# A two-stage attention and channel mixer: half of one weight matrix converted during the first batch's products, and one maximum on GpSimd

## The chip, the cores and the metric

The kernel runs on one core of a Trainium2 chip. A core has a matrix engine (PE, with its own weight loader), a vector engine (DVE), a scalar engine (ACT), a general engine (POOL, called GpSimd in the code), and SyncE (SP), whose queue issues the transfers here. The metric is device time in microseconds, the median of three timed runs. One more execution is recorded by the hardware profiler; all rows in this document are from such executions.

## What is computed

For each of 8 batches and 8 heads, 32 packed queries `p` attend over 576 keys and values of width 64; the packed result then serves as keys and values for 576 queries `q`. The eight heads side by side give x of 576 tokens by 512 channels. A low-rank mixer adds a term over the tokens, and a two-layer network over the channels follows:

```python
p_packed = sm_attn(p, k, v)
out = sm_attn(q, p_packed, p_packed)
xt = x.transpose(0, 2, 1)
h = xt @ U @ V
u = x + h.transpose(0, 2, 1)
ch = np.maximum(u @ w_ch1, 0.0) @ w_ch2
return u + ch
```

`w_ch1` (w1, 512 by 2048) and `w_ch2` (w2, 2048 by 512), U and V come as float64; the others are float32.

## The kernel before, in words

**Two parts.** The front part (up to line 541) runs the first attention for all batches in 16 units, one for each batch and half of the heads, the second attention of batch 0, and the conversion of all of w1. Its instructions are put in order by a planner that simulates the program and takes, for each engine, what is ready by its costs; instructions traced earlier have precedence. From line 544 on, `tc.manual_schedule()` keeps the order in which the code is written, engine by engine. There, a loop over batches `b` and 16 row blocks `kt` of the hidden layer runs `gemm1(kt)` and then `gemm2(kt - 1)`, and hangs the other work between them. Each engine takes its instructions strictly in the order given.

**Products.** Every float32 factor is split into two parts, and a product is three matmuls (`mm3`, lines 84 to 88). `gemm1` does not multiply by w1 itself: `fold(b, c)` (line 355) first multiplies a quarter of w1's columns by the packed attention of batch b, into tiles `wth`, `wtl`. That takes 16 matmuls into two banks of the two-bank pool `psT`, four ACT copies (L367) and four DVE subtractions (L368). Quarter c = 0 of batch 0 is folded at unit 13, and quarters 1, 2, 3 in the loop at the end of kt = 2, 6, 10; quarter c needs the four converted chunks 4c to 4c + 3 of w1. The two banks are also used by the attention steps and by the leftover steps `rest` of the front part, so a PE step that needs a bank waits until L368 has read the fold's. `gemm1` evicts with ACT (`hh`, L596, and `hj`, L598) and DVE (`hl`, L599); its two banks are single, so `gemm1(kt + 1)` waits for the `hl` of kt.

**Conversion of float64.** `float32_of` (line 71) makes float32 from the two 32-bit words: an absolute value on ACT (L77, or L143 in `test_w1`), a maximum against a constant on DVE (L78), and three DVE instructions on bits: a shift and mask (L79), and two that combine it with the words (L80, L81). w1 comes in 16 chunks of 128 by 512 (512 KB each), loaded by `load_w1`, tested by `test_w1` and converted by `convert_w1`; in the front part one chunk goes with each unit, and two with units 1, 5 and 9. w2 comes in 16 blocks of the same size: blocks 0 to 2 are loaded in the front part, one more is loaded, converted and split (L158 on ACT, L159 on POOL) with each kt of batch 0 up to kt = 13. The tiles of a conversion, `os`, are four in all, shared by w1 and w2.

**Second attention.** `attention(b, res)` is a list of 24 steps: a load of q (two transfers of 576 KB into the two `x` tiles), turns (PE transposes, copies from PSUM half by ACT and half by DVE), scores, softmax (DVE maximum L267, POOL subtraction L268, ACT exponential L271, DVE sum L276, POOL product L279, DVE transpose L283), tokens, and the mixer (`mix1`, `mix2`). In the loop of batch b the steps of batch b + 1 are popped, one after `gemm1` and one at the end of a kt; at kt % 4 == 2 the fold takes the second place. Batch 1's load is issued in the front part, at unit 13; `rest` has the first place in kt = 0 to 3.

Of the kernel before, what the change touches and what calls it, by code (L numbers as in the profile page):

```python
# [19 lines left out]
def packed_attention_mixer_kernel(  # L20
# [27 lines left out]
    nc = tc.nc  # L48
# [22 lines left out]
    def float32_of(x, t, raw, out=None, tested=False):  # L71


        low, high = raw[:, :, 0], raw[:, :, 1]
        out = x if out is None else out.bitcast(I32)
        if not tested:
            nc.scalar.activation(t, high.bitcast(F32), AF.Abs)  # L77
        nc.vector.tensor_single_scalar(t, t, LEAST, op=ALU.max)  # L78
        nc.vector.tensor_scalar(x, t.bitcast(I32), 3, 0x3FFFFFF8, op0=ALU.logical_shift_left, op1=ALU.bitwise_and)  # L79
        nc.vector.scalar_tensor_tensor(x, high, -0x40000000, x, op0=ALU.bitwise_and, op1=ALU.bitwise_or)  # L80
        nc.vector.scalar_tensor_tensor(out, low, 29, x, op0=ALU.logical_shift_right, op1=ALU.bitwise_or)  # L81
        return out.bitcast(F32)
# [47 lines left out]

    chunks = [(x, c) for c in range(NPC) for x in range(4)]
# [9 lines left out]
    def test_w1(n):  # L141
        tests[n] = conv_tile(F32)
        nc.scalar.activation(tests[n], bits["w1", n][:, :, 1].bitcast(F32), AF.Abs)  # L143

# [20 lines left out]

    def x_tile():
        return pipe.tile([P, 5 * 2 * P], F32, name="x", tag="x", bufs=2)
# [32 lines left out]

    def turn(t, x, h, bank):
# [3 lines left out]
        if h < 2:  # L205
# [4 lines left out]
            for a in range(2):  # L210
                dst = t[:, 2 * h:2 * h + 2, :4 * I].rearrange("p z (k i a) -> p a z k i", k=2, a=2)[:, a]
                if a:
                    nc.vector.tensor_copy(dst, src[:, a])
                else:
                    nc.scalar.copy(dst, src[:, a])
# [25 lines left out]
    def attention(b, res):  # L241
# [11 lines left out]
        def turn_q(g, h):  # L253
            if h == 0:
                st["t", g] = pipe.tile([P, 4, 5 * I], F32, name="xT", bufs=1)
            turn(st["t", g], st["x", g], h, bank)
# [240 lines left out]
    n_w1 = 0  # L497
    for i in range(NU):
# [42 lines left out]
    actx.close()  # L541

# [19 lines left out]
    class Batch:  # L562
# [39 lines left out]
        def gemm2(self, kt):  # L602
# [3 lines left out]
            for t in range(4):  # L606
                ts_ = slice(t * P, t * P + P)
# [54 lines left out]

    w2x = convert_w2(1)
    last, parts = None, []
    for b in range(B):
# [3 lines left out]
        for kt in range(NK):  # L669
            cur.gemm1(kt)  # L670
            if oj and kt == 1:
                store_joint(b - 1, oj)
            if rest:
                rest.pop(0)()
            elif steps and (b == 0 or kt % 4 != 2):
                steps.pop(0)()
            if (b, kt) == (0, 5):
                w2_tiles(ctx.enter_context(tc.tile_pool(name="sC", bufs=1, side="right", reuse_waits="tile")), 2)
            if kt > 0:
                cur.gemm2(kt - 1)  # L680
# [5 lines left out]
            if w2x:  # L686
# [57 lines left out]
```

## Time and profile before

| | |
|---|---|
| median of 3 runs | 881.36 us (880.0 to 882.8) |
| the profiled execution's own time | 877.17 us |
| its span, first to last instruction | 875.2 us |
| mean granted clock of PE | 0.973 |
| PE busy | 836.0 us, 96% |
| DVE busy | 402.6 us, 46% |
| ACT busy | 322.8 us, 37% |
| POOL busy | 95.0 us, 11% |
| read from memory, written | 47.79 MB, 10.35 MB |

In a row of a timeline stand the start in us, the duration in us, the engine, the line, the operation and the tiles, and in brackets how long the engine was idle before and what ended that. A row of a table by stage gives the busy time of each engine within the stage with the count of its instructions, then PE's granted clock, the busy share of the transfer engines, and what these moved. A row of groups gives the total and the mean ns of one instruction. PE shows busy when its pipeline is filled, so a PE near 100% is not PE at its peak.

### The profile page before, as it was taken

The page shows a single profiled execution, that of the slowest core. Times are in us where ns is not written, and L with a number is a line of the kernel's source. Part 1 is how long each engine was busy: PE and PEld are TensorE (multiplying, and loading weights), DVE is VectorE, ACT ScalarE, POOL GpSimd, SP SyncE. Part 2 cuts the span into 40 slices and gives each one's busy share as a digit, 9 for nine tenths or more (in the row PEclk, how much of TensorE's full clock was granted, in tenths as well). Part 3 has the DMA queues.
Part 4 walks back from the last instruction along what each step waited for, and adds up shares of the span by engine and source line. Part 5 has one row for each costly group of instructions (what it writes and reads, how often), then busy time and mean ns, then how long its engine had stood idle before and what let it go on. Part 6 is the DMA issues. An engine that isn't in the chain of part 4 may idle for free.

```text
span 875.2 us, 14665 instructions
## 1 busy us (share of the span) xinstructions
PE 836.0 (96%) x5808; PEld 665.1 (76%) x5808; DVE 402.6 (46%) x988; ACT 322.8 (37%) x1000; POOL 95.0 (11%) x111
## 2 busy tenths in 40 slices
PE   5878899979999999999999999999999999999997
PEld 2554557858888888788878878888888887888886
DVE  4699757876433323433443433434343334332221
ACT  3666564534322333234223332233223332332221
POOL 0002222323001100100010000110011001010000
PEclk8799799989999999999999999999999999999999
DMA  8999833322100110011001100011001100010001
GB/s 273 290 337 292 278 115 102 95 75 85 49 1 1 61 53 10 1 61 49 1 1 61 49 13 1 1 61 49 1 1 61 48 13 1 1 49 1 1 1 60
DMA packets 38979, 59.08 MB, mean 68 GB/s; under 512 B 11776, under 2 KB 21888, under 8 KB 38912
## 3 DMA queue, kind: packets, MB, share of 16 engines
q1 hardware_dynamic: 38912, 58.16, 20.4%
q8 instruction: 45, 0.74, 0.4%
q14 instruction: 22, 0.18, 0.1%
HBM read 47.79 MB, written 10.35 MB: 66 GB/s over the span
## 4 chain that ended last, share of the span: by engine, by line
PE 85%; DVE 7%; DMA 4%; issue 1%; ACT 1%; POOL 0%; SPq 0%; ACTq 0%; DVEq 0%; POOLq 0%
PE o L86 16%; PE o L88 16%; PE o L87 16%; PE h_ps L86 8%; PE h_ps L88 7%; PE h_ps L87 7%; PE t_ps L361 4%; DMA bits<-in_moe_w_ch_dram 2%; PE t_ps L208 1%; DVE os L80 1%; PE t_ps L229 1%; PE s_ps L229 1%; PE t_ps L304 1%; PE t_ps L236 1%; DMA x<-in_moe_U_dram 1%
## 5 line engine op out<-in xcount | busy, mean ns | idle before, releaser
L86 PE MATMUL o<-w2h,hh 128*128 128x512 f32 x512 | 208.7, 408 | 0.0
L88 PE MATMUL o<-w2h,hl 128*128 128x512 f32 x512 | 203.5, 397 | 0.0
L87 PE MATMUL o<-w2l,hh 128*128 128x512 f32 x512 | 203.0, 397 | 0.0
L599 DVE SCALAR_TENSOR_TENSOR hl<-h_ps,hh 128x256 fp32r<-128x256 f32 x256 | 104.4, 422 | 167.2 <-ACT hj L598 154.4
L596 ACT ACTIVATE hh<-h_ps 128x256 fp32r<-128x256 f32 x256 | 98.9, 388 | 188.9 <-PE h_ps L88 188.1
L86 PE MATMUL h_ps<-ah,wth 128*128 128x320 f32 (+1 forms) x512 | 158.2, 309 | 1.2 <-DVE hl L599 1.2
L87 PE MATMUL h_ps<-al,wth 128*128 128x320 f32 (+1 forms) x512 | 151.6, 296 | 0.0
L88 PE MATMUL h_ps<-ah,wtl 128*128 128x320 f32 (+1 forms) x512 | 151.4, 296 | 0.0
L86 PEld LDWEIGHTS h_ps<-ah,wth 128*128 128x128 f32 x512 | 96.9, 189 | 32.7 <-issue 25.7
L88 PEld LDWEIGHTS o<-w2h,hl 128*128 128x128 f32 x512 | 97.1, 190 | 23.1
L86 PEld LDWEIGHTS o<-w2h,hh 128*128 128x128 f32 x512 | 97.4, 190 | 22.2 <-issue 4.1
L87 PEld LDWEIGHTS o<-w2l,hh 128*128 128x128 f32 x512 | 97.6, 191 | 17.4
L87 PEld LDWEIGHTS h_ps<-al,wth 128*128 128x128 f32 x512 | 97.0, 189 | 1.9
L88 PEld LDWEIGHTS h_ps<-ah,wtl 128*128 128x128 f32 x512 | 97.0, 190 | 0.0
L368 DVE TENSOR_TENSOR wtl<-t_ps,wth 128x256 fp32r<-128x256 f32 x128 | 48.5, 419 | 93.9 <-ACT wth L367 90.5
L367 ACT CAST wth<-t_ps 128x256 fp32r<-128x256 f32 x128 | 43.4, 374 | 109.1 <-PE t_ps L361 97.1
L324 POOL TENSOR_TENSOR al<-aT,ah 128x320 fp32r<-128x320 f32 (+1 forms) x32 | 26.2, 818 | 211.6 <-ACT ah L323 211.6
L268 POOL TENSOR_TENSOR e<-e,m 128x576 f32<-128x576 f32 x16 | 19.6, 1226 | 237.8 <-DVE m L267 232.4
L361 PE MATMUL t_ps<-w1t,ppT 64*32 64x512 f32 x512 | 36.5, 601 | 0.0
L323 ACT CAST ah<-aT 128x320 fp32r<-128x320 f32 (+1 forms) x32 | 13.9, 433 | 52.8 <-DVE aT L322 52.8
L279 POOL TENSOR_TENSOR e<-e,s 128x576 f32<-128x576 f32 x16 | 18.9, 1179 | 110.3 <-DVE s L278 106.4
L296 DVE TENSOR_TENSOR x<-t_ps,x 128x512 fp32r<-128x512 f32 (+1 forms) x24 | 14.3, 599 | 32.6 <-ACT x L295 32.6
(130 smaller groups left out, 1021.9 us busy)
## 6 DMA issues: line engine op xcount, KB each, us to landing
bits<-in_moe_w_ch_dram SPq DMA_DIRECT2D x32, 512.0 KB, 4.9
kx<-in_k_dram SPq DMA_DIRECT2D x16, 576.0 KB, 6.1
x<-in_q_dram SPq DMA_DIRECT2D x16, 576.0 KB, 4.8
vt<-in_v_dram SPq DMA_DIRECT2D x64, 128.0 KB, 4.9
out_dram<-bits SPq DMA_DIRECT2D x32, 256.0 KB, 2.4
pn<-in_p_dram SPq DMA_DIRECT2D x16, 64.0 KB, 5.6
vt<-in_v_dram SPq DMA_DIRECT2D x16, 64.0 KB, 4.2
out_dram<-os SPq DMA_DIRECT2D x8, 128.0 KB, 2.3
```

Of the source, the lines that this page charges most:

```text
L86: nc.tensor.matmul(ps, lhsT=lh, rhs=rh, start=start, stop=False)
L87: nc.tensor.matmul(ps, lhsT=lh, rhs=rl, start=False, stop=False)
L88: nc.tensor.matmul(ps, lhsT=ll, rhs=rh, start=False, stop=stop)
L229: nc.tensor.matmul(ss[r][hs, :n], lhsT=lT[rs, g, hs], rhs=t[rs, h, :n], start=True, stop=True)
L268: nc.gpsimd.tensor_tensor(e, e, m.unsqueeze(2).to_broadcast([P, S // 32, 32]), op=ALU.subtract)
L279: nc.gpsimd.tensor_tensor(e, e, s.unsqueeze(2).to_broadcast([P, S // 32, 32]), op=ALU.mult)
L324: nc.gpsimd.tensor_tensor(al[:, g, ns], aT[:, ns], ah[:, g, ns].bitcast(F32), op=ALU.subtract)
L361: nc.tensor.matmul(f_ps[g][xs], lhsT=ppT[b][zs, g, xs], rhs=w1t[h // 2][zs, QW * c:QW * c + QW], start=True, stop=True)
L367: nc.scalar.copy(hi[:, g], f_ps[g][:, cs])
L368: nc.vector.tensor_tensor(lo[:, g], f_ps[g][:, cs], hi[:, g].bitcast(F32), op=ALU.subtract)
L596: nc.scalar.activation(hh[:, ms], src, AF.Relu)
L599: nc.vector.scalar_tensor_tensor(hl[:, ms], src, 0.0, hh[:, ms].bitcast(F32), op0=ALU.max, op1=ALU.subtract)
```

## The change

Chunks 0 to 7 of w1 (column quarters 0 and 1) stay in the front part, one with every second unit. The loads of chunks 8 to 10 are traced at unit 14; chunks 8 to 15 are converted in the loop of batch 0 by `late_w1`, two each at kt = 0, 2 and 4 and one each at kt = 1 and 3. They are loaded into tiles that the second attention uses, the two `x` tiles and `xT`, so the q load of batch 1 comes after them. Batch 1's attention starts, load and all, when the last chunk is converted, at the end of kt = 4, and has three places in each kt then (after `gemm1`, in the middle of `gemm2`, at the end), two where a fold stands. The maximum of all 16 chunks of w1 goes from DVE to GpSimd, behind the absolute value. In the loop, both PSUM copies of a turn are on ACT.

```diff
         if not tested:
             nc.scalar.activation(t, high.bitcast(F32), AF.Abs)
-        nc.vector.tensor_single_scalar(t, t, LEAST, op=ALU.max)
+            nc.vector.tensor_single_scalar(t, t, LEAST, op=ALU.max)
...
+    EARLY = 8
...
     def load_w1(n):
         x, c = chunks[n]
-        b = bits["w1", n] = bits_tile() if n % 2 else sA.tile([P, 512, 2], I32, name="bits2")
+        if n < EARLY:
+            b = bits_tile() if n % 2 else sA.tile([P, 512, 2], I32, name="bits2")
+        else:
+            b = xT_tile().rearrange("p h x -> p (h x)") if (n - EARLY) % 3 == 2 else x_tile()
+            b = b[:, :2 * QW].bitcast(I32).rearrange("p (x t) -> p x t", t=2)
+        bits["w1", n] = b
...
         nc.scalar.activation(tests[n], bits["w1", n][:, :, 1].bitcast(F32), AF.Abs)
+        nc.gpsimd.tensor_single_scalar(tests[n], tests[n], LEAST, op=ALU.max)
...
-                if a:
+                if a and split_copies:
                     nc.vector.tensor_copy(dst, src[:, a])
                 else:
                     nc.scalar.copy(dst, src[:, a])
...
     def some_w1(n):
         convert_w1(n)
-        if n + 1 < 16:
+        if n + 1 < EARLY:
             test_w1(n + 1)
-        if n + 4 < 16:
+        if n + 4 < EARLY:
             load_w1(n + 4)
...
-        for _ in range(2 if i in (1, 5, 9) else 1):
-            if n_w1 < 16:
-                some_w1(n_w1)
-                n_w1 += 1
+        if i % 2 == 1:
+            some_w1(i // 2)
...
         if i == 13:
             fold(0, 0)
-            steps = attention(1, res)
-            steps.pop(0)()
         if i == 14:
             split_w2(*convert_w2(0))
             load_w2(2)
+            for n in range(EARLY, EARLY + 3):
+                load_w1(n)
...
+    split_copies = False
...
-        def gemm2(self, kt):
+        def gemm2(self, kt, between=None):
...
             for t in range(4):
+                if t == 2 and between:
+                    between()
...
+    def late_w1():
+        nonlocal n_w1
+        n = n_w1
+        convert_w1(n)
+        for m, f in ((n + 1, test_w1), (n + 3, load_w1)):
+            if m < len(chunks):
+                f(m)
+        n_w1 += 1
+
+    n_w1 = EARLY
+    test_w1(n_w1)
     w2x = convert_w2(1)
+    steps = attention(1, res)
...
+            def step():
+                if steps and (b > 0 or n_w1 == len(chunks)):
+                    steps.pop(0)()
+
             cur.gemm1(kt)
...
             if rest:
                 rest.pop(0)()
-            elif steps and (b == 0 or kt % 4 != 2):
-                steps.pop(0)()
+            elif b == 0 or kt % 4 != 2:
+                step()
+            if b == 0 and kt < 5:
+                late_w1()
...
             if kt > 0:
-                cur.gemm2(kt - 1)
+                cur.gemm2(kt - 1, step if b == 0 else None)
...
+            if b == 0 and kt in (0, 2, 4):
+                late_w1()
             if kt % 4 == 2 and (b, kt) != (B - 1, NK - 2):
                 n = b * NPC + kt // 4 + 1
                 fold(n // NPC, n % NPC)
-            elif steps:
-                steps.pop(0)()
+            else:
+                step()
```

More of the change, by code (lines that the diff above doesn't have):

```diff
@@ L129, in bits_tile, with x_tile, xT_tile @@
         return pipe.tile([P, 512, 2], I32, name="bits", bufs=2)
+    def x_tile():
+        return pipe.tile([P, 5 * 2 * P], F32, name="x", tag="x", bufs=2)
+    def xT_tile():
+        return pipe.tile([P, 4, 5 * I], F32, name="xT", bufs=1)
     chunks = [(x, c) for c in range(NPC) for x in range(4)]
+    EARLY = 8
     bits = {}
@@ L164, in packed_attention_mixer_kernel @@
     vs = const.tile([P, S], F32R, name="vs")
-    def x_tile():
-        return pipe.tile([P, 5 * 2 * P], F32, name="x", tag="x", bufs=2)
     def load_uv():
@@ L199, in load_nat @@
             in_=src[b, 4 * g:4 * g + 4].rearrange("(h z) (i c) d -> (z i) h (c d)", z=2, c=NT))
+    split_copies = True
     def turn(t, x, h, bank):
@@ L254, in turn_q @@
             if h == 0:
-                st["t", g] = pipe.tile([P, 4, 5 * I], F32, name="xT", bufs=1)
+                st["t", g] = xT_tile()
             turn(st["t", g], st["x", g], h, bank)
@@ L491, in some_w1 @@
         convert_w1(n)
-        if n + 1 < 16:
+        if n + 1 < EARLY:
             test_w1(n + 1)
-        if n + 4 < 16:
+        if n + 4 < EARLY:
             load_w1(n + 4)
-    n_w1 = 0
     for i in range(NU):
```

## The prediction

> **What bounds the kernel now.** I read the busy time by stage first, and then the chain of waits inside the stage that looked worst.
>
> ```profile
> core 0: us, PE busy (x) PEld busy (x) DVE busy (x) ACT busy (x) POOL busy (x), PEclk, DMA share, GB/s
> 0.00:120.00 120.00, 94.12 (x1121) 56.12 (x1121) 88.03 (x242) 70.42 (x214) 16.86 (x30) 0.84 0.88 277
> 40.00:80.00 40.00, 32.16 (x476) 20.74 (x473) 37.77 (x104) 26.35 (x79) 6.56 (x8) 0.92 0.96 309
> 100.00:110.00 10.00, 6.62 (x57) 4.74 (x55) 8.30 (x16) 5.70 (x19) 4.97 (x5) 0.72 0.91 290
> 122.00:208.00 86.00, 79.07 (x581) 64.76 (x571) 64.15 (x129) 41.13 (x116) 24.51 (x26) 0.96 0.32 104
> 420.00:520.00 100.00, 99.73 (x614) 81.78 (x612) 37.89 (x93) 31.74 (x100) 7.87 (x8) 1.00 0.08 27
> ```
>
> There are three regimes. In the front part (0 to 122) two things are full at once in the middle: DVE with 37.77 of 40 us, and the transfers with a share of 0.96 at 309 GB/s. PE is idle for 26 of the first 120 us and runs at a clock of 0.84. In batch 0 (122 to 208 is its kt = 0 to 14) PE is idle for 7 us and DVE is 75% busy. From batch 1 on PE has 99.73 of 100, and nothing beside PE matters.
>
> So the change takes work from a stage where DVE and the transfers bound, and puts it into one where PE nearly bounds but where DVE's queue already stops it now and then. The first stage's chain, from 60 to 125, with one of its stretches in order of time (start, duration, what):
>
> ```profile
> by line: PE s_ps L229 12.0%; DMA bits<-in_moe_w_ch_dram 11.6%; DVE os L80 7.4%; PE m_ps L236 6.1%; PE k_ps L208 5.6%; DVE w1t L81 5.3%; DVE mx L433 5.1%; PE m_ps L463 5.1%; DVE os L79 4.3%; DVE os L78 4.0%; DVE kT L213 3.3%; DMA ppTd<-ppTa
> 93.86 7.54 DMA bits<-in_moe_w_ch_dram
> 101.42 0.67 ACT os L77
> 105.96 0.73 DVE mx L433 x2
> ```
>
> The conversions (L78 to L81) hold 21.0% of these 65 us, 13.7 us. From 93.86 on the chain is the load of w2's block 1 and its conversion; the maximum of the next unit (105.96) stands behind it on DVE.
>
> **The front part: what goes.** The groups, by shape, from 0 to 260; one row on the turns of k (ns of one at least, in the middle and at most, first and last start); and two transfer rows (size, us to landing):
>
> ```profile
> L80 DVE SCALAR_TENSOR_TENSOR os<-bits,os 128x512 int32<-128x512 int32 x32 | 23.9, 746 | 0.6
> L78 DVE TENSOR_SCALAR os<-os 128x512 f32<-128x512 f32 x32 | 20.9, 653 | 12.5 <-ACT os L77 8.5 <-ACT os L143 3.8
> L79 DVE TENSOR_SCALAR os<-os 128x512 int32<-128x512 int32 x32 | 15.4, 480 | 1.4
> L81 DVE SCALAR_TENSOR_TENSOR w1t<-bits,os 128x512 int32<-128x512 int32 x16 | 11.4, 713 | 0.0
> L143 ACT ACTIVATE os<-bits 128x512 f32<-128x512 f32 x16 | 10.9, 678 | 7.9 <-DMA bits<-in_moe_w_ch_dram 6.1 <-DVE w1t L81 0.9 <-DVE mx L433 0.7
> L159 POOL TENSOR_TENSOR w2l<-os,w2h 128x512 fp32r<-128x512 f32 x16 | 21.0, 1315 | 39.3 <-ACT w2h L158 39.3
> L466 POOL COPY ppall<-two 128x64 f32<-128x64 f32 x16 | 5.9, 368 | 82.7 <-ACT two L465 82.7
> L208 PE MATMUL k_ps<-ident,kx x128: 272/273/475, 5.9 to 109.7; 128*128 128x128 f32 x128
> bits<-in_moe_w_ch_dram SPq DMA_DIRECT2D x32, 512.0 KB, 4.9
> x<-in_q_dram SPq DMA_DIRECT2D x16, 576.0 KB, 4.8
> ```
>
> Eight chunks leave: 8 x 512 KB = 4.19 MB, at the 0.30 MB per us of the stage 14.0 us of transfer time. On DVE they are 8 x (0.653 + 0.480 + 0.746 + 0.713) = 20.7 us, and the maxima of the eight that stay are 8 x 0.653 = 5.2 us more. Both full resources get more than 14 us, so the smaller, the transfers, says 14. To this comes a second part. `test_w1(8)` now stands ahead of `convert_w2(1)` on ACT, and its load comes last in the front part, so w2's block 1 is converted later, where DVE is free: the chain loses the 4.5 us from 101.42 to 105.96. That makes 18.5. Batch 1's q load also leaves (2 x 576 KB), but behind the last k it delayed nothing on the chain, and I give it 0; if it did delay something, it would be 1.18 MB, 3.9 us.
>
> The bounds: at least half of the conversions' 13.7 us in the chain, so 7. At most what PE allows: it is idle for 26 us, some 6 of these before the first turn (5.9), so 20. I take **17**, near what the transfers say. The three late loads at unit 14 come when the share has fallen and cost nothing; in front of the last units they would cost 3 x 0.52 / 0.30 = 5.2 us (the last rival).
>
> The GpSimd maximum is not in the trace. It reads one tensor of 512 columns: more than the copy of 64 columns (0.368), less than the subtraction of two tensors of 512 (1.315). I take the middle, 0.8. In the front part POOL has 103 of 120 us free, which hides 8 x 0.8; what it costs in batch 0 comes below.
>
> **Batch 0, kt = 0 to 3.** Rows of PE (the first `gemm1` and its end, two `gemm2` with their ends, the waits, and the `gemm1` of kt = 6 and 14), then of DVE:
>
> ```profile
> 122.36 0.42 PE L86 MATMUL h_ps<-ah,wth 128*128 128x320 f32 x1
> 124.15 0.90 PE L463 MATMUL t_ps<-vt,eT 128*32 128x64 f32 x40
> 129.34 0.48 PE L86 MATMUL o<-w2h,hh 128*128 128x512 f32 x1
> 132.18 0.60 PE L208 MATMUL t_ps<-ident,x 128*128 128x128 f32 x4
> 141.63 0.30 PE L473 MATMUL t_ps<-ident,two 128*128 128x128 f32 x1 [0.59 <-DVE wtl L368]
> 158.04 0.39 PE L86 MATMUL h_ps<-ah,wth 128*128 128x320 f32 x1
> 184.78 0.41 PE L86 MATMUL h_ps<-ah,wth 128*128 128x320 f32 x1 [1.23 <-DVE hl L599]
> 190.46 1.08 PE L236 MATMUL t_ps<-ident,aT 128*128 128x128 f32 x4 [3.83 <-DVE wtl L368]
> 191.20 0.77 PE L86 MATMUL o<-w2h,hh 128*128 128x512 f32 x1
> 196.47 0.62 PE L236 MATMUL t_ps<-ident,aT 128*128 128x128 f32 x4
> 208.12 0.38 PE L86 MATMUL h_ps<-ah,wth 128*128 128x320 f32 x1
> ```
>
> ```profile
> 125.36 0.75 DVE L599 SCALAR_TENSOR_TENSOR hl<-h_ps,hh 128x256 fp32r<-128x256 f32 x2 [3.35 <-ACT hj L598]
> 127.13 1.06 DVE L78 TENSOR_SCALAR os<-os 128x512 f32<-128x512 f32 x1 [1.02 <-ACT os L77]
> 132.80 0.43 DVE L79 TENSOR_SCALAR os<-os 128x512 int32<-128x512 int32 x1
> 133.99 0.69 DVE L81 SCALAR_TENSOR_TENSOR os<-bits,os 128x512 int32<-128x512 int32 x1
> 134.60 0.42 DVE L213 COPY xT<-t_ps 128x256 f32<-128x256 f32 x1
> 140.20 1.61 DVE L368 TENSOR_TENSOR wtl<-t_ps,wth 128x256 fp32r<-128x256 f32 x4
> 149.30 0.96 DVE L599 SCALAR_TENSOR_TENSOR hl<-h_ps,hh 128x256 fp32r<-128x256 f32 x2 [2.91 <-ACT hj L598]
> ```
>
> DVE is without a gap from 125.36 to the fold's last subtraction at 141.81, but for 1.02. In PE's order the leftover step of kt = 3 (L473) needs one of the two banks that the fold of kt = 2 holds, and waits for that subtraction (0.59); `gemm2(2)` stands behind it. Whatever is put on DVE ahead of it shifts PE. The change puts chunks 8 to 12 there: L79 to L81 take 1.88 (132.80 to 134.68), so 9.4. Two xT copies leave for ACT (0.34 each from start to start), and the 1.02 is filled: +7.7. Two unknowns come on top. There are four `os` tiles, so an absolute value for w2 may find none free until a conversion ends; DVE then waits for one ACT instruction (0.678) in each of three kt, 0 to 2.0. And GpSimd's five maxima can hold DVE up:
>
> ```profile
> 168.23 1.21 POOL L279 TENSOR_TENSOR e<-e,s 128x576 f32<-128x576 f32 x1 [5.78 <-DVE s L278]
> 168.53 1.19 DVE L79 TENSOR_SCALAR os<-os 128x512 int32<-128x512 int32 x1
> ```
>
> L79, otherwise 0.43, ended 0.28 after POOL's instruction. So one maximum that meets such an instruction costs up to its length, 0 to 5 x 0.8 = 4.0 in all. I take 9.5 of 7.7 to 13.7, as only some will meet. (The Trainium skill, "SBUF — State Buffer", section "SBUF: two separate sides", calls the port pair that DVE and GpSimd share an exclusive lock, held for the whole instruction. By that rule, with each maximum meeting, these three kt would be at 11.7 plus the tile waits instead of 9.5; the row here agrees with a lock, but shows one meeting, not how many there will be.)
>
> PE then stands idle for some 7 us in one piece. After 3.83 idle the four triples of a `gemm2` took 5.27 (191.20 to 196.47) instead of 2.84 (129.34 to 132.18): a slow clock costs **2.4** more, 0 if the clock holds.
>
> **kt = 4 and 5.** Chunk 13 fits DVE's 2.91 of idle time before 149.30. Chunks 14 and 15 go while PE has `gemm2(3)` and `gemm1(5)`. But the q load of batch 1 needs the tile that chunk 14 leaves: 1.88 + 4.8 after the `hl` of kt = 4, when PE reaches the first turn after 2.84 + 1.8 (a `gemm1`, 122.36 to 124.15). It waits **2**, between 0 and 3. So kt = 6 comes 14 us later, counted from the first `gemm1`. On SP's queue w2's blocks stand behind the loads of w1 and q, each of which waits for a DVE conversion that is earlier in DVE's order than its user; no cost by itself.
>
> **kt = 6 to 14.** Before: 158.04 to 208.12, 50.1 us, with 16 steps of attention. After, 20 steps fall in it. Four turns more on PE are 4 x 0.5 = **2**; the DVE copies are gone. The stall before `tokens` (1.23, 3.83 and the slow clock) stays in kind: maximum, subtraction, exponential and sum now follow one another in kt = 9 with a conversion of w2 between, and `tokens` in kt = 10 waits in the middle of a `gemm2`. Worse by between 0 and one conversion (2.6 by the groups above): I take **2**. With the ends of all terms, batch 0 loses between 10 and 24; my sum is 9.5 + 2.4 + 2 + 2 + 2 = **18**.
>
> **Later batches.** Both turn copies on ACT: 2 x 2 x 0.4 us each batch under a PE that has 99.73 of 100, with ACT at 31.74. No cost; without that cover it would be 1.6 a batch.
>
> **The sum**, against the profiled execution's own 877.2 (its span 875.2): -17 + 18 = +1, so 878. The median of the runs is 4.2 above that execution, which makes **882**.
>
> **The rivals.**
> *Faster (873).* DVE is idle for 22 of 86 us in batch 0; if tile and port waits don't come and the clock holds, only some 11 is lost, and the front part gives its full 20: -9. Against it: the idle time of DVE lies after 142, not where the conversions are put.
> *Slower by the shared port (889).* In kt = 0 to 4 each of the eight maxima blocks DVE for its 0.8, and the tile waits come, too: batch 0 loses 24, +7. It decides from the point where POOL's maximum regularly starts while DVE is in L78 to L81, which here fill most of DVE's time.
> *Slower, as the front part is not freed (893).* PE, at 94 of 120 us busy with a clock of 0.84, and the order of each unit bound instead: the front part gives only 7, so -7 + 18 = +11. Against it: the share of 0.96.
> *The late loads aren't late (888).* The planner issues them as soon as tiles are free, ahead of the last units' v: 17 - 5 = 12, so +6.
>
> **How the numbers follow.** Forecast 0.30 (own range 877 to 887), faster 0.36, port 0.16, front part 0.14, early loads 0.04. A measurement tells about 0.3%, 2.6 us, from no change, so "same" is 878.7 to 884.0: 0.20 of the forecast and 0.04 from the others' edges, 0.24. Faster: 0.34 and 0.02 of the forecast, 0.36. Slower: the rest, 0.40. The range that leaves 2 in 10 out reaches past the faster rival and the slowest one: 869 to 894.
>
> **What would show it.** Right: the first `gemm1` at about 105; a PE wait of several us before L473 of kt = 3, ended by DVE's L368; 103 to 104 us from the first `gemm1` to that of kt = 14 (85.8 before); a wait of about 7 us before `tokens` in kt = 10; PE full from batch 1 on. Wrong: a first `gemm1` after 112 or before 101, or a batch 0 under 98 us; L79 to L81 well over 1.88 in kt = 0 to 4 speaks for the port.

## The result, and the profile after

The changed kernel takes **893.47 us** (median of 4 runs, 893.27 to 894.39), the kernel before beside it on the same chip 881.01. The ratio on record, taken from the runs of both kernels, is **1.0157, interval 1.0134 to 1.0181**; the two medians alone give 1.0141. The profiled execution took 893.4, its span is 891.6. The forecast was 882, no change. Its range, 869 to 894, just holds the time.

The busy time by stage of the changed kernel. The stages are the start of the front part, its rest up to the first `gemm1`, kt = 0 to 5, kt = 6 to 13, and 100 us of batches 3 and 4:

```profile
0.00:18.00 18.00, 9.44 (x59) 5.04 (x59) 5.36 (x13) 7.30 (x18) 5.08 (x10) 0.92 0.82 265
18.00:115.68 97.68, 85.92 (x1117) 51.58 (x1116) 66.62 (x196) 59.40 (x192) 24.25 (x34) 0.82 0.83 256
115.68:165.93 50.25, 37.02 (x277) 30.75 (x271) 40.72 (x73) 22.87 (x65) 22.63 (x20) 0.86 0.46 146
165.93:225.74 59.81, 47.47 (x296) 36.62 (x293) 41.90 (x77) 23.16 (x61) 16.81 (x15) 0.94 0.26 90
420.00:520.00 100.00, 99.72 (x621) 82.27 (x620) 37.87 (x92) 34.83 (x109) 8.61 (x9) 1.00 0.10 35
```

The same stages of the kernel before, cut at its own first `gemm1` (122.36), kt = 6 (158.04) and kt = 14 (208.12):

```profile
0.00:18.00 18.00, 8.76 (x48) 4.46 (x48) 6.40 (x18) 7.61 (x18) 0.85 (x7) 0.93 0.81 264
18.00:122.36 104.36, 87.72 (x1131) 52.95 (x1127) 83.19 (x231) 63.75 (x198) 18.37 (x29) 0.83 0.88 277
122.36:158.04 35.68, 33.81 (x300) 28.09 (x295) 25.90 (x56) 18.84 (x59) 10.18 (x12) 1.00 0.34 107
158.04:208.12 50.08, 45.02 (x270) 36.59 (x268) 38.36 (x73) 22.03 (x57) 14.09 (x12) 0.93 0.30 100
```

Line them up. The front part loses 17.6 us of DVE work (89.6 to 72.0) and becomes 6.7 us shorter. PE is busy in it for as long as before, 95.4 us against 96.5. Batch 0 up to kt = 14 takes 110.06 instead of 85.76: 14.6 more in kt = 0 to 5, 9.7 more in kt = 6 to 13. From kt = 14 to the end of the span nothing is lost (665.9 and 667.1). So -6.7 + 24.3 - 1.2 = 16.4, the difference of the spans.

The long waits of PE in batch 0 of the changed kernel, with the `gemm1` of kt = 0, 2, 6, 10 and 14, from PE's rows in order of time:

```profile
115.68 0.42 PE L86 MATMUL h_ps<-ah,wth 128*128 128x320 f32 x1
127.15 0.43 PE L86 MATMUL h_ps<-ah,wth 128*128 128x320 f32 x1 [3.60 <-DVE hl L610]
144.46 0.44 PE L486 MATMUL t_ps<-ident,two 128*128 128x128 f32 x1 [6.07 <-DVE wtl L381]
160.50 0.66 PE L221 MATMUL t_ps<-ident,x 128*128 128x128 f32 x4 [2.37 <-DMA x<-in_q_dram]
165.93 0.39 PE L86 MATMUL h_ps<-ah,wth 128*128 128x320 f32 x1
191.65 0.42 PE L86 MATMUL h_ps<-ah,wth 128*128 128x320 f32 x1 [1.73 <-DVE hl L610]
202.01 0.90 PE L249 MATMUL t_ps<-ident,aT 128*128 128x128 f32 x3 [7.00 <-DVE aT L296]
225.74 0.41 PE L86 MATMUL h_ps<-ah,wth 128*128 128x320 f32 x1 [0.87 <-DVE hl L610]
```

L381, L486 and L610 are L368, L473 and L599 of the kernel before. The wait of 6.07 at the leftover step of kt = 3 and the one of 2.37 for batch 1's q are those forecast. The wait of 7.00 before `tokens` is the one that was expected, too, but shorter ones stand beside it. What stands ahead of it on ACT, DVE and POOL:

```profile
193.93 0.69 ACT L284 ACTIVATE e<-e 128x576 f32<-128x576 f32 x1 [6.38 <-POOL e L281]
194.52 0.60 ACT L172 CAST w2h<-os 128x512 fp32r<-128x512 f32 x1
195.03 0.65 ACT L77 ACTIVATE os<-bits 128x512 f32<-128x512 f32 x1
...
195.72 1.03 DVE L78 TENSOR_SCALAR os<-os 128x512 f32<-128x512 f32 x1 [3.13 <-ACT os L77]
...
198.65 0.74 DVE L289 TENSOR_REDUCE s<-e 128x18 f32<-128x576 f32 x1
...
199.99 1.16 POOL L292 TENSOR_TENSOR e<-e,s 128x576 f32<-128x576 f32 x1 [3.52 <-DVE s L291]
201.18 0.78 DVE L296 STREAM_TRANSPOSE aT<-e 128x576 f32<-128x576 f32 x1 [0.67 <-POOL e L292]
```

The rows left out on DVE between 195.72 and 199.99 are L79 to L81, two small steps of the softmax and two evictions of `gemm1`; the others are other work of ACT and POOL. The exponential is done at 194.62. Its sum (L289) starts at 198.65, since in DVE's order a conversion of w2 (L78 to L81) stands ahead of it, and that conversion waits 3.13 for its own absolute value, which stands on ACT behind the exponential and a cast. DVE idles with the sum's input ready, and PE idles behind DVE.

### The profile page after: what moved, and what is told of

Its sections match the earlier page's. It is cut to its first block, busy times and chain, and to the rows that moved or that the text cites. A ratio compares the mean times of both kernels' runs of the same rounds, so it can differ in the third digit from the quotient of the medians.

```text
span 891.6 us, 14662 instructions
## 1 busy us (share of the span) xinstructions
PE 839.4 (94%) x5808; PEld 666.4 (75%) x5808; DVE 392.8 (44%) x944; ACT 330.2 (37%) x1028; POOL 119.3 (13%) x127
## 4 chain that ended last, share of the span: by engine, by line
PE 84%; DVE 7%; DMA 3%; ACT 2%; issue 2%; POOL 1%; SPq 0%; ACTq 0%; DVEq 0%; POOLq 0%
PE o L86 16%; PE o L88 15%; PE o L87 15%; PE h_ps L86 8%; PE h_ps L88 7%; PE h_ps L87 7%; PE t_ps L374 3%; PE t_ps L221 2%; PE k_ps L221 2%; PE s_ps L242 1%; DVE os L80 1%; PE t_ps L242 1%; PE t_ps L317 1%; DMA kx<-in_k_dram 1%; PE m_ps L476 1%
## 5 line engine op out<-in xcount | busy, mean ns | idle before, releaser
L610 DVE SCALAR_TENSOR_TENSOR hl<-h_ps,hh 128x256 fp32r<-128x256 f32 x256 | 104.1, 422 | 201.2 <-ACT hj L609 188.7
L381 DVE TENSOR_TENSOR wtl<-t_ps,wth 128x256 fp32r<-128x256 f32 x128 | 48.4, 419 | 92.0 <-ACT wth L380 88.6
L228 ACT COPY xT<-t_ps 128x256 f32<-128x256 f32 x60 | 20.4, 392 | 42.8 <-PE t_ps L221 42.1
```

The source lines that it names most:

```text
L381: nc.vector.tensor_tensor(lo[:, g], f_ps[g][:, cs], hi[:, g].bitcast(F32), op=ALU.subtract)
L610: nc.vector.scalar_tensor_tensor(hl[:, ms], src, 0.0, hh[:, ms].bitcast(F32), op0=ALU.max, op1=ALU.subtract)
```

## The experiments

All edits are to the kernel before or to the changed one, as each says. "Of before" is the ratio to the kernel before, run beside it.

Where a first `gemm1` is given, it comes from one trace, and such a figure scatters. The run with the turn copies alone (below) has the same code in its front part as the kernel before, and its first `gemm1` is at 125.06, where that of the kernel before is at 122.36. Two traces with all of w1 and its maxima on GpSimd have it at 119.26 and 122.19, two of the changed front part at 115.68 and 116.56. Differences of up to 3 us between single traces show nothing by themselves.

**One part at a time.** First, the changed kernel with w1's maxima back on DVE:

```diff
-        nc.gpsimd.tensor_single_scalar(tests[n], tests[n], LEAST, op=ALU.max)
...
-            nc.vector.tensor_single_scalar(t, t, LEAST, op=ALU.max)
+        nc.vector.tensor_single_scalar(t, t, LEAST, op=ALU.max)
```

> The changed kernel with one part undone: w1's maximum is on DVE again (L78 for all chunks), nothing runs on GpSimd for it. Theory Q (DVE's queue: the eight conversions ahead of the fold's subtractions in kt = 0 to 4, and the attention squeezed into kt = 5 to 13, are the loss): in the changed kernel GpSimd's maxima stretched DVE's instructions by some 3.5 us between the first hl and the fold of kt = 2, while five DVE maxima would take 2.2 there, so batch 0 stays over 104 us (109 measured) and the time is 890 to 893. Theory P (the shared port: a GpSimd maximum takes 1.52 us, and each holds DVE or its data up): batch 0 falls to under 100, the front part ends before 110, and the time is under 884.

Measured 900.25, 1.0223 of before (1.0188 to 1.0258), slower than either theory said. The maxima on GpSimd are worth 5.8 us to the changed kernel (0.0066 of 880); the rival of the shared port, which made them a loss, falls.

The maxima on GpSimd alone, in the kernel before:

```diff
+        nc.gpsimd.tensor_single_scalar(tests[n], tests[n], LEAST, op=ALU.max)
```

> The kernel before with one part of the change alone: the maximum of w1's 16 chunks on GpSimd, all chunks still in the front part. Theory Q: DVE is relieved of 16 x 0.43, GpSimd is free in the front part, so 879 to 883. Theory P: 16 x 1.52 us on the port, against a DVE that is full from 40 to 80 us, lengthens the front part; 886 or more.

Measured 875.6, 0.9934 of before (0.9908 to 0.9959): a gain of 5.8 us here too, more than either theory said, although one maximum takes twice what was assumed.

Batch 1's attention alone moved behind kt = 4, with three places per kt, w1 left whole in the front part:

```diff
-            steps = attention(1, res)
-            steps.pop(0)()
...
+    steps = attention(1, res)
...
+            def step():
+                if steps and (b > 0 or kt >= 5):
+                    steps.pop(0)()
...
-                cur.gemm2(kt - 1)
+                cur.gemm2(kt - 1, step if b == 0 else None)
```

> The kernel before with one part alone: batch 1's attention, its load of q too, starts at the end of kt = 4 of batch 0 and has three places in each kt then; w1 is all in the front part, the maximum on DVE, the turn copies shared by ACT and DVE. Theory Q, with both of its parts of like size: the wait for q (2.4), the stall in kt = 9 to 10 (1.7 and 7.0 where it was 1.2 and 3.8) and the later steps cost 6 to 10, so 887 to 891. If the late conversions alone are the loss: 879 to 883. If the squeezed attention alone is the loss: 893 or more.

Measured 892.59, 1.0133 of before (1.0098 to 1.0168). Its `gemm1` of kt = 0, 6 and 14 and the wait before `tokens`, from PE's rows:

```profile
124.99 0.42 PE L86 MATMUL h_ps<-ah,wth 128*128 128x320 f32 x1
162.31 0.39 PE L86 MATMUL h_ps<-ah,wth 128*128 128x320 f32 x1
200.22 0.90 PE L236 MATMUL t_ps<-ident,aT 128*128 128x128 f32 x3 [6.99 <-DVE aT L283]
223.95 0.41 PE L86 MATMUL h_ps<-ah,wth 128*128 128x320 f32 x1 [0.87 <-DVE hl L597]
```

The time lies between two of the forecasts, 887 to 891 and 893 or more. kt = 6 to 14 takes 61.6 instead of 50.1, with the same wait of 7 us before `tokens`, and no late chunk is converted anywhere. So the late attention alone costs 11.7 us by the ratio, and the loss in kt = 6 to 13 of the changed kernel is there without any of the late conversions.

The changed kernel with maxima on DVE, but without the late chunks: they are neither loaded nor converted, their columns of w1 are zeros, so half of the first layer's products are of zeros.

```diff
+    for x in range(4):
+        nc.gpsimd.memset(w1t[x][:, DF // 2:], 0.0)
...
     def late_w1():
...
-        convert_w1(n)
-        for m, f in ((n + 1, test_w1), (n + 3, load_w1)):
-            if m < len(chunks):
-                f(m)
```

> The changed kernel without the late chunks: columns 1024 to 2047 of w1 are zeros written once, their loads, tests and conversions are left out, so the product with them is left out in effect; the maximum is on DVE; batch 1's attention still starts at the end of kt = 4. It shows the front part with half of w1 by itself, and batch 0 without the late conversions. Theory Q: batch 0 takes 92 to 96 us from the first gemm1 to that of kt = 14 (85.8 before, 109 changed). For the front part: if PE's slow clock and the order of the units bound it, the first gemm1 comes at 112 to 116 (115.7 in the changed kernel, 122.4 before) and the time is 880 to 884; if GpSimd's maxima had held it up, at 104 to 108, and the time is 872 to 877.

Measured 881.39, 1.0016 of before (0.9987 to 1.0044). Against the first run the eight late conversions cost 18 us (0.0207 of 880), and all of it in kt = 0 to 5, which takes 34.6 here and 54.1 there. So there are two losses, the late conversions in kt = 0 to 5 and the late attention behind them, and the first is the larger. And with half of w1 gone for good, the first `gemm1` is at 117.35, only 5 us earlier than in the trace of before (7.7 against the one at 125.06), and 0.4 earlier than in the first run (117.78), which has the late loads.

Both turn copies on ACT in the loop, alone, in the kernel before:

```diff
-                if a:
+                if a and split_copies:
...
+    split_copies = False
```

> The kernel before with only one part of the change: both copies of a turn on ACT inside the loop (in the front part one half stays on DVE). By the prediction nothing: PE covers ACT in batches 1 to 7, and in batch 0 DVE loses 8 x 2 copies of about 0.34 that do not lie ahead of a wait of PE: 879 to 883, first gemm1 to kt = 14 in 84 to 86. If the two copies one after the other on ACT hold a turn up, each of the turns adds 0.4 in the batches: 16 x 0.4 = 6 and more, 885 to 890.

Measured 878.02, 0.997 of before (0.9949 to 0.9992): no cost, perhaps a small gain. From the first `gemm1` to kt = 14 it takes 85.96, as forecast.

**What held the front part?** The kernel before without w1: no load, no test, no conversion, zeros in its place.

```diff
+    for x in range(4):
+        nc.gpsimd.memset(w1t[x], 0.0)
...
-    for n in range(4):
-        load_w1(n)
...
-            if n_w1 < 16:
-                some_w1(n_w1)
-                n_w1 += 1
```

> The kernel before with w1 left out: its columns are zeros written once on GpSimd, nothing of it is loaded, tested or converted, so the result lacks the network's product. It shows what the front part costs without any of w1. The first gemm1 came at 122.4 before, at 115.7 to 117.8 in the kernels with half of w1 there. If transfers and DVE bound the front part (as the prediction had it), the 8.4 MB less give 28 us of transfer time and it comes at 95 to 100. If PE bounds it, by the order of the units and a clock of 0.6 to 0.8 while it shows busy, it comes at 108 to 116, no more than as much again as the first half gave.

Measured 853.79, 0.9713 of before (0.9684 to 0.9742); the first `gemm1` is at 99.05, 23 earlier. This is the answer that was expected if transfers and DVE bound the front part (95 to 100), not the one for PE (108 to 116): w1 as a whole does hold it. But the two halves are not worth the same. Taking the second half out gave 5 to 8; the first half is worth 18 more (117.35 to 99.05).

The kernel before, w1's chunks 8 to 15 loaded and their absolute values taken, but not converted on DVE (these columns are zeros):

```diff
-        convert_w1(n)
+        if n < 8:
+            convert_w1(n)
```

> The kernel before without DVE's four instructions for chunks 8 to 15 (their columns are zeros written once, so the result lacks their product); all 16 loads and absolute values stay in the front part. If the transfers held the front part, the first gemm1 stays at 120 to 122; if DVE did, it comes at 115 to 118, as with loads and conversions gone; if PE does, in between.

Measured 875.76, 0.9948 of before (0.9922 to 0.9975), first `gemm1` at 118.15. With all the transfers there, the front part is 0.8 longer than without them (117.35), less than such traces scatter: no gain from the transfers that leave can be seen. The 18.1 us of work that leave DVE (89.6 to 71.5 up to the first `gemm1`) are worth 4.2 us here (6.9 against the trace at 125.06).

The changed kernel with PE filled: two more matmuls, whose results nothing uses, in each of units 2 to 8.

```diff
+        if 2 <= i <= 8:
+            w_ps = bank()
+            for _ in range(2):
+                nc.tensor.matmul(w_ps, lhsT=ident, rhs=ua[i]["x"][:, :512], start=True, stop=True)
         a_scores(i)
```

> The changed kernel with two more matmuls in each of units 2 to 8 of the front part (128x128 by 512 columns, f32, identity times k), whose results nothing uses. They add some 14 matmuls of about 0.6 to 0.9 us, 9 to 13 us of PE time, and take nothing from DVE, ACT or the transfers. If the clock that stays at 0.50 for 24 us holds the front part (theory), the fuller PE brings the clock up earlier: mean clock from 30 to 60 at 0.75 or more, first gemm1 at 104 to 112 instead of 115.68, time 882 to 890. If it is the order and latency of the units, or PE's plain work, the first gemm1 comes 3 to 13 later, at 118 to 128, and the time is 896 to 905. Batch 0 is as in the changed kernel (110 from the first gemm1 to kt = 14) in both cases.

Measured 903.94, 1.0281 of before (1.0235 to 1.0327), first `gemm1` at 125.01: the second answer. In the stretch in which the clock of the changed kernel was 0.50 it is 0.82 here, but that does not pay for the work that was added. The stretch in the changed kernel, then in this one, and the front part of this one:

```profile
33.00:56.00 23.00, 21.52 (x208) 12.49 (x207) 16.60 (x49) 10.92 (x30) 5.30 (x6) 0.50 0.95 300
```

```profile
33.00:56.00 23.00, 20.80 (x225) 11.16 (x225) 19.91 (x60) 14.06 (x46) 7.21 (x7) 0.82 0.78 243
0.00:18.00 18.00, 9.22 (x59) 4.85 (x59) 5.12 (x12) 7.18 (x18) 4.88 (x10) 0.94 0.84 263
18.00:125.01 107.01, 95.65 (x1148) 54.35 (x1144) 67.62 (x197) 59.57 (x195) 26.27 (x37) 0.84 0.78 236
```

PE is busy for 104.9 us of 125.0, so idle for 20.1; in the changed kernel it was busy for 95.4 of 115.7, idle for 20.3. The other kernels with half of w1 and the old order of loads idle for 19.4 to 20.3 as well. So the 9.5 us that PE is busy longer appear one for one in the time of the front part: in this kernel PE's time plus a nearly fixed idle time sets its end. A clean test of the clock it is not: the added matmuls are busy for 17.3 us by themselves, where 9 to 13 were expected, and as they read k, PE's waits for k grow from 3.3 to 6.8 us.

What is that idle time? The queue SP of the changed kernel, first rows (start, duration of the issue, what is loaded):

```profile
6.08 2.03 SPq L150 DMA_DIRECT2D bits<-in_moe_w_ch_dram  x4
8.16 3.13 SPq L416 DMA_DIRECT2D vt<-in_v_dram  x4
...
16.60 0.37 SPq L208 DMA_DIRECT2D kx<-in_k_dram  x1
```

The first four chunks of w1 are issued at 6.08 (6.15 in the kernel before), before unit 1's v and unit 2's k. Two waits of PE go back to them:

```profile
12.60 0.66 ACT L156 ACTIVATE os<-bits 128x512 f32<-128x512 f32 x1 [2.53 <-DMA bits<-in_moe_w_ch_dram]
...
14.70 0.54 ACT L450 ACTIVATE e<-s_ps,mx 128x320 f32<-128x320 f32 x1
...
15.38 0.47 PE L249 MATMUL m_ps<-ident,e 128*128 128x128 f32 x1 [3.29 <-ACT e L450]
...
21.59 1.94 PE L221 MATMUL k_ps<-ident,kx 128*128 128x128 f32 x8 [2.11 <-DMA kx<-in_k_dram]
```

PE waits 2.11 for unit 2's k. And it waits 3.29 for unit 0's exponential (L450), whose maxima DVE has done at 12.00: on ACT it stands behind the absolute values of w1's chunks 0 and 1, the first of which waits 2.53 for its load. So the order was changed:

```diff
-    for n in range(4):
-        load_w1(n)
     a_turn(0)
...
-    test_w1(0)
...
             a_load(i + 2)
+        if i == 0:
+            for n in range(4):
+                load_w1(n)
+            test_w1(0)
```

> The changed kernel with one order changed: the first four loads of w1 (2.1 MB, 7 us at 0.30 MB per us) and the first absolute value stand behind unit 1's v and unit 2's k instead of ahead of everything. Theory: the changed kernel's front part is PE's own work (95 of 115.68 us) behind a start of 18 us in which PE is idle for 8.6 and waits for p, k and v; then PE starts earlier, first gemm1 at 109 to 113 instead of 115.68, time 886 to 891, and batch 0 as before (about 110). Rival: the start does not matter, as what PE gains there it loses waiting for w1's quarters or for softmax later: first gemm1 at 115 to 118, time 891 to 896.

Measured 886.54, 1.0080 of before (1.0051 to 1.0108), against 1.0157 for the changed kernel. Its queue with unit 0's exponential on ACT, and its stages up to the first `gemm1`:

```profile
10.55 0.47 SPq L208 DMA_DIRECT2D kx<-in_k_dram  x1
11.06 2.27 SPq L150 DMA_DIRECT2D bits<-in_moe_w_ch_dram  x4
...
12.63 0.52 ACT L450 ACTIVATE e<-s_ps,mx 128x320 f32<-128x320 f32 x1
```

```profile
0.00:18.00 18.00, 11.39 (x68) 6.63 (x69) 3.88 (x12) 6.97 (x20) 1.45 (x8) 1.00 0.83 261
18.00:107.30 89.30, 81.39 (x1108) 48.67 (x1106) 67.52 (x196) 58.91 (x189) 26.82 (x35) 0.89 0.89 279
```

Unit 2's k is issued 6 us earlier and unit 0's exponential starts 2 us earlier. PE idles 14.5 us instead of 20.3, and is busy for 92.8 instead of 95.4, at a granted clock of 1.00 and 0.89 instead of 0.92 and 0.82. The first `gemm1` comes 8.4 us earlier by the order of two groups of loads and one absolute value; batch 0 gives 1.3 of that back (111.39 to kt = 14). Nothing was taken from any resource. The theory of the late start holds; 109 to 113 was even too little. How much of it is the wait for k, and how much the exponential's, this edit does not divide.

**The blocks of w2 taken ahead, and the order of loads in the kernel before.** The kernel before with w1's maxima on GpSimd, w2's blocks loaded one kt earlier, and their absolute value and maximum (GpSimd) one kt ahead of the conversion; then the same treatment of w2 in the changed kernel:

```diff
+    def test_w2(kt):
+        t = tests["w2", kt] = conv_tile(F32)
+        nc.scalar.activation(t, bits["w2", kt][:, :, 1].bitcast(F32), AF.Abs)
+        nc.gpsimd.tensor_single_scalar(t, t, LEAST, op=ALU.max)
...
-                if kt + 3 < NK:
-                    load_w2(kt + 3)
...
+                if kt + 4 < NK:
+                    load_w2(kt + 4)
+                if kt + 3 < NK:
+                    test_w2(kt + 3)
```

> The kernel before with the maximum of w1 on GpSimd, and in batch 0 the blocks of w2 treated in the same way: loaded one kt earlier, the absolute value on ACT and the maximum on GpSimd one kt ahead of DVE's conversion. It takes L78 off DVE's queue and the absolute value out from behind the softmax's exponential. Theory Q (DVE's queue in batch 0 is what stops PE): the waits of 1.2 and 3.8 us in kt = 11 shrink below 2 in all and batch 0 falls from 88 to 82 to 85, so 869 to 873. If the chain of the softmax itself makes the stall, or GpSimd's 14 maxima of 1.5 us hold the port: 876 or more.

> The changed kernel with w2's blocks loaded and tested one kt ahead, their maxima on GpSimd. Theory Q: DVE sheds 5 x 0.43 and the waits for ACT in kt = 0 to 4, and in kt = 9 the conversion no longer waits behind the exponential; the stall of 7.0 before tokens becomes 4 to 5 and batch 0 falls from 110 to 102 to 106, so 885 to 889. If the port decides here, where GpSimd gets 13 maxima of 1.5 us in kt = 0 to 4 beside its other work: 893 or more.

Measured 873.05 for the first, 0.9929 of before (0.9910 to 0.9948), batch 0 in 82.3 us from the first `gemm1` to kt = 14, as forecast. By the ratio this is no more than the maxima of w1 alone gained (0.9934); that the treatment of w2 adds to it shows in the trace only. For the second 892.25, 1.0177 (1.0127 to 1.0227), no better than the changed kernel: the wait before `tokens` shrinks from 7.00 to 4.82, and the one for q grows from 2.37 to 6.65. The end of the late chunks on the queue SP, in the changed kernel and then in this one:

```profile
145.61 6.03 SPq L165 DMA_DIRECT2D bits<-in_moe_w_ch_dram  x2
156.71 5.56 SPq L208 DMA_DIRECT2D x<-in_q_dram  x2
```

```profile
150.77 9.80 SPq L165 DMA_DIRECT2D bits<-in_moe_w_ch_dram  x2
160.66 2.16 SPq L214 DMA_DIRECT2D x<-in_q_dram  x2
```

A load of w2 that is held until 160.57 now stands ahead of q's, which is issued 4 us later. kt = 0 to 5 takes 54.65 instead of 50.25; kt = 6 to 13 takes 53.10 instead of 59.81, with PE idle for 5.8 us in it instead of 12.3. Of the 6.7 us gained behind kt = 6 the later q takes 4.4 back, and the other 2.3 don't stand clear of noise in the time.

The filler in the first of these, and then the order of loads in it:

> The kernel before with w1's maxima on GpSimd and w2 loaded and tested one kt ahead (873.05 in an earlier run), and the same unused matmuls in units 2 to 8. Theory that the clock matters in the front part: here transfers and DVE are full too, so little is gained: first gemm1 at 116 to 122 instead of 122.19, time 868 to 874. Theory that the added PE work only delays: first gemm1 at 124 to 132, time 875 to 884.

Measured 874.8, 0.9943 (0.9920 to 0.9966), first `gemm1` at 121.64 (122.19 without): the added work costs nothing here that could be seen, and gains nothing. PE is busy for 101.1 us instead of 98.2, and idle for 20.5 instead of 24.0: with all of w1 in the front part the added work goes into idle time. That PE's time sets the end is so in the changed kernel, not here.

```diff
             a_load(i + 2)
+        if i == 0:
+            for n in range(4):
+                load_w1(n)
+            test_w1(0)
...
-        for _ in range(2 if i in (1, 5, 9) else 1):
-            if n_w1 < 16:
+        for _ in range(2 if i in (3, 5, 7, 9) else 1):
+            if 0 < i and n_w1 < 16:
```

> The kernel before with w1's maxima on GpSimd and w2 one kt ahead (873.05), and in the front part the first four loads of w1 behind the k and v loads of the first units, conversions from unit 1 on, two each with units 3, 5, 7 and 9. If the start of the front part waits for k and v behind w1's loads, the units start earlier by up to 4 x 512 KB at 0.30 MB per us, 7 us: first gemm1 at 115 to 120, time 866 to 871. If DVE's total decides, no change: 871 to 875; if the conversions now bunch behind the units, later: 875 to 880.

Measured **867.72**, 0.9877 of before (0.9843 to 0.9910), first `gemm1` at 117.79: 4.4 earlier than without (1.5 against the trace at 119.26), and the best time of all. The same with both turn copies on ACT:

> The kernel before with w1's maxima on GpSimd, w2 one kt ahead, w1's first loads behind k and v (867.72 in an earlier run), and both turn copies on ACT in the loop. If the turn copies are covered, as in the run with them alone (0.997 of before), 865 to 869; if ACT now sets the end of a turn in batch 0, 870 to 874.

Measured 868.46, 0.9871 (0.9830 to 0.9912): no difference from the one before.

## Why the prediction was wrong

**The front part, -17, measured -6.7 (-9.4 against the trace at 125.06): the step that failed.** It said that the transfers and DVE both bound the stage, that both get more than 14 us, and that "the smaller, the transfers, says 14", with 4.5 more from the chain. Sizing the gain by what the fullest resources lose took for granted that nothing else held the stage's end. Half of w1 taken out altogether gives 5 to 8 (first `gemm1` 117.35), and nearly as much with its transfers left in (118.15). The share of 0.96 that seemed to speak against a late release was read from 40 to 80, where the transfers were full with loads whose absence changed little. The place where a transfer was seen to set the pace is the start, where four chunks of w1 are issued ahead of unit 2's k and one of their absolute values stands ahead of an exponential: chunks that the change leaves where they are. Behind that, PE's own time counts: the same number of matmuls (1176 up to the first `gemm1`) took 95.4 us in the changed kernel, and 1178 took 82.7 without w1. There neither k nor an exponential stands behind w1, though PE's first matmul waits until 6.5 for the identity, which GpSimd makes behind the zeros:

```profile
0.00:18.00 18.00, 8.65 (x69) 5.41 (x69) 4.17 (x13) 6.63 (x20) 7.82 (x11) 1.00 0.78 234
18.00:99.05 81.05, 74.02 (x1109) 44.72 (x1105) 52.84 (x170) 54.10 (x182) 15.72 (x28) 0.98 0.85 260
```

Of the 16.6 us between 115.68 and 99.05, 12.7 are longer PE work at a clock of 0.82 instead of 0.98 and 3.9 are idle time. My bound "at most what PE allows, 20" came from PE's idle time in the kernel before; of that, only 5.6 went away (25.9 to 20.3). How much of the 12.7 an early start brings by itself, and how much lies in w1's remaining work on DVE, ACT and the transfers, the runs don't divide: the changed order gives 2.6 of it. So it is shown that the fullest resources did not size the gain, and that the start costs 7 to 8 us (8.4 in the trace, 6.8 by the ratio); what makes the rest of the first half's 18 us stays open.

**kt = 0 to 3, +9.5, measured +9.5.** From the first `gemm1` to the leftover step of kt = 3 it was 141.63 - 122.36 = 19.27, and is 144.46 - 115.68 = 28.78. The sum is right, and to the tenth by luck, as its largest unknown was wrong: a maximum takes 1.6 us, not 0.8. L79 to L81 of the five chunks take 11.1 us from start to start, 2.2 each instead of 1.88, which was named as a sign of the port. The groups of POOL by shape, 0 to 260, in the changed kernel:

```profile
L157 POOL TENSOR_SCALAR os<-os 128x512 f32<-128x512 f32 x16 | 26.0, 1626 | 45.0 <-ACT os L156 45.0
L173 POOL TENSOR_TENSOR w2l<-os,w2h 128x512 fp32r<-128x512 f32 x16 | 21.4, 1338 | 29.9 <-ACT w2h L172 29.9
```

It reads one tensor and takes longer than the subtraction of two, which was thought to be the upper bound. And the two engines do meet, in rows of POOL and DVE in the order of time:

```profile
119.68 1.55 POOL L157 TENSOR_SCALAR os<-os 128x512 f32<-128x512 f32 x1 [0.43 <-ACT os L156]
121.20 1.47 POOL L173 TENSOR_TENSOR w2l<-os,w2h 128x512 fp32r<-128x512 f32 x1
121.55 1.41 DVE L79 TENSOR_SCALAR os<-os 128x512 int32<-128x512 int32 x1
...
127.55 1.49 POOL L157 TENSOR_SCALAR os<-os 128x512 f32<-128x512 f32 x1 [2.52 <-ACT os L156]
127.79 0.65 DVE L79 TENSOR_SCALAR os<-os 128x512 int32<-128x512 int32 x1
```

The first L79, otherwise 0.43, again ends 0.3 after POOL's instruction. (The Trainium skill, "SBUF — State Buffer", section "SBUF: two separate sides", calls the shared port pair an exclusive lock; the rows up to 121.55 agree.) The second starts inside a maximum on GpSimd, takes 0.65 and ends 0.6 before it, so not every meeting lasts until GpSimd is done. The first meeting costs a microsecond, and yet the maxima on GpSimd gain 5.8 in either kernel. In the changed one each takes 0.65 off a DVE that is busy for 25.3 of the 26.5 us from 118 to the fold's end. In the kernel before, whose w1 is all in the front part, the runs don't show where the gain arises. With the maxima back on DVE, kt = 0 to 14 takes 113.78 instead of 110.06, and the front part 2.1 more.

**kt = 4 and 5, +4.4, measured +5.1** (50.25 - 35.68 = 14.57 for kt = 0 to 6, less 9.5). The q wait was to be 2 and is 2.37. The clock is 0.86 in kt = 0 to 5 (1.00 before), as the slow clock's 2.4 assumed. Right in sum and in both signs.

**kt = 6 to 14, +4, measured +9.7: mis-sized.** PE's work grew by 2.45 (45.02 to 47.47), where 2 was said. Its idle time grew by 7.3 (5.06 to 12.34), where 2 was said, "between 0 and one conversion (2.6)". The wait before `tokens` grew by 3.2, from 3.83 to the 7.00 that the prediction had named as a sign. The bound missed that the conversion ahead of the sum can itself be waiting: its absolute value stands on ACT behind the exponential. The other 4.1 are short waits that the sum had at nothing: 1.93 at a turn in kt = 7 that nothing in the profile explains, 0.87, 0.51 and 0.30, and 1.73 where there was one of 1.23. Most of all this hangs on w2's conversions: with their absolute values and maxima one kt ahead, PE idles for 5.8 us in kt = 6 to 13. The run with the late attention alone has the same 7 us and is a little longer there (61.6), so it needs no late w1 work. In all, batch 0 lost 24.3, just past the end of 24 that the prediction's terms allowed.

**Later batches, 0: right.** 665.9 from kt = 14 against 667.1; the turn copies alone cost nothing.

**The offset.** I added 4.2 because the profiled execution of before lay that far under its median. The changed kernel's profiled execution lies on its median (893.40 and 893.47), so of the 16.2 between the profiles 12.5 remain between the medians. The run with the turn copies alone suggests where the profiled execution of before was quick: its front part, of the same code, is 2.7 longer (125.06), and its kt = 0 to 14 are not (85.96 and 85.76).

**The rivals.** Slower, as the front part is not freed (893, chance 0.14): its -7 is what happened, and PE at a low clock was its reason. The added matmuls, which also held k longer, don't settle that reason. It still had batch 0 at +18 where it was 24.3; that its 893 is the measured time is two errors that cancel, the 6.3 missing and the 4.2 of the offset. The shared port (889) falls by the run with the maxima back on DVE, which is slower. Faster (873) wanted 20 from the front part and a loss of 11 in batch 0; neither is near. The late loads: two are issued at 96.23, ahead of the last units' v, as that rival said:

```profile
96.23 1.06 SPq L150 DMA_DIRECT2D x<-in_moe_w_ch_dram  x2
97.38 2.50 SPq L416 DMA_DIRECT2D vt<-in_v_dram  x4
```

No wait of PE for v shows in the front part, and without these loads the first `gemm1` is not clearly earlier (117.35 against 117.78, both with the maxima on DVE), so they cost nothing that can be seen.

## What to carry to other kernels

What a stage gains from work taken out of it is not what its fullest resource loses; ask which instruction waited for that resource, and what the stage would be limited by next: here PE's own time behind a late start. Reordering two groups of loads shortened the changed kernel's front part by 8.4 us, as much as taking half of the conversions out of it had done. When work is pushed later, count what it pushes in turn: the attention squeezed out of kt = 0 to 4, alone, cost 11.7 us, more than the whole front part gained. And a wait is bounded by the waits of everything that stands ahead of it in the same queue, on its own engine and on the one that feeds it, not by the duration of one piece of that work.

## What the runs showed of the hardware

PE ran at a granted clock of 0.50 for 23 us (33 to 56 of the changed kernel) while it showed busy for 21.52 of them. Part of the work there are turns against an identity; those of k take 0.425 us each (0.27 in the middle, before), by the group row of that stretch:

```profile
L221 PE MATMUL k_ps<-ident,kx 128*128 128x128 f32 x24 | 5.8, 425 | 0.0
```

(The Trainium skill, "TensorE: Matmul & The Clock Gate", Part 1, has the clock full after about 3.4 us of sustained work. Its Part 4 says that transposes don't count as busy in the same way.) By the first alone such a stretch would not last, with the second it can. But turns alone don't make it: without w1 the same stretch holds 32 turns of k, at 278 ns each, under a clock of 1.00. Nor is the figure the front part's own: the changed kernel with w2 ahead, whose front part has the same code, is granted 0.63 there. With two plain matmuls more in each of units 2 to 8 it was 0.82. What holds the clock down stays open.

In the profile of the run with these matmuls added the granted clock stands at 0.95 through all batches instead of 1.00, and the time from kt = 14 (237.23) to the end of its span of 904.0 is 666.8, against 665.9. The matmuls of `gemm2` take as long there, 406, 394 and 395 ns for the three of a product from 420 to 520, against 407, 395 and 396 in the changed kernel. So a granted clock that is 5% lower in the record does not show in PE's work here, while the 0.50 above does, in the turns of k.
